# Decode attention on one core: value products into one set of 32 rows, key pieces and value tiles as register loops, the last values in four loads

## The chip, the cores and the metric

The kernel runs on one core of one Trainium2 chip. The metric is the device time of one execution in microseconds (us). A core has five engines that run their own instruction queues and meet at semaphores: PE (matrix products), DVE (vector work), ACT (activations), POOL and SP (here SP only issues transfers, DMAs). PE writes its results to PSUM, a memory of its own, from which DVE and ACT read; the other tiles lie in SBUF.

## The reference, cut to what matters

One token passes a layer of attention over a long cache and then a small MLP. The attention has 32 query heads that share 8 key-value heads (four each), a cache of 16384 tokens, and heads of 128 values, in bf16:

```python
q = (x @ wq).reshape(B, Sq, Hq, Dh).transpose(0, 2, 1, 3)
k = jnp.repeat(k_cache, rep, axis=1)
v = jnp.repeat(v_cache, rep, axis=1)
scores = jnp.einsum("bhqd,bhkd->bhqk", q, k) * (Dh ** -0.5)
p = _softmax(scores, axis=-1)
o = jnp.einsum("bhqk,bhkd->bhqd", p, v)
return o.transpose(0, 2, 1, 3).reshape(B, Sq, Hq * Dh) @ wo
```

`x` is layer-normalised ahead of it and added behind it; the MLP (`w3`, GELU, `w4`) has its own layer norm and its own addition. With one token the shifts in the reference's mixing step leave only zeros, so `w1` and `w2` have no part. The keys and values are 67 MB together, all of which has to be read once; the weights make the rest of the 79 MB.

## The kernel before, in words

**The pairs.** The 8 key-value heads are worked through in 4 pairs (`PAIRS`, L257; the loop at L590). The keys of a pair (8 MB) go to `kb`, in two halves of 64 tokens per partition; its values (8 MB) go to `vb`. Each of these buffers exists once. Partition 64g + u holds 256 neighbouring tokens of head g of the pair.

**Scores.** For each half, DVE transposes the keys from `kb` into `kt` in 8 pieces (`transpose_keys`, L516, the instruction at L520), and PE makes 4 products for each piece (`scores`, L525, L528): 128 columns of a widened query tile `qn` against 512 key columns. A later piece takes the window of `qn` that is shifted by 4 columns, so each piece lands on rows of its own of `s_ps[:, y, :]`, y being the half. PE waits for DVE's count before each piece. The second half's transposes write over the first half's `kt`, piece by piece, once PE has read it.

**Softmax.** `softmax` (L536): DVE takes the maxima (L539), PE turns them (L540), DVE and PE make the bias, ACT computes the exponentials with their sums in `acc` (L550), and DVE transposes these into `pt` (L554, two instructions).

**Values.** `values` (L557) has 64 products (L562): 32 columns of `pt` against 4 tokens x 128 values. Four neighbours (`ct` 0 to 3) go to rows 0, 32, 64 and 96 of one PSUM tile `O_ps[0]`, each over its own 32 columns of the array; 16 such groups are summed up. All wait for the pair's values and for `pt`.

**Gather.** `gather` (L567): a product makes the sums of the exponentials (L570), DVE picks the right block for each row with four masked steps over 128 rows (L575, L578), a product folds them (L581), and DVE divides (L583, L584) into `o_m`.

**Transfers.** All large ones are issued by SP, in the order of the program: `wq`, keys 0, values 0, then for each pair the next keys (pair 1's in one transfer, the others in halves, each once DVE has transposed the half that it overwrites) and the next values (L604, once the last value product has read `vb`). `wo` goes to the first half of `kb`, `w3` and `w4` to the second, after the last keys. The queue serves them in that order.

**PE's program.** Every operation is recorded with its dependencies (`Program.op`, L43), and waits are made from them. DVE, ACT, POOL and SP run their lists straight through (`_run`, L128). PE's list is emitted as a loop over the pairs (`_tensor`, L136): a block for a half, run twice with register `ry` as the half, and a block `pe_rest` for softmax, values and gather. In a half, the 8 pieces with their 32 products are written out one after the other, with a register addition and a wait ahead of each piece (L211), and the branch back at L218. The 64 value products are written out too, behind one wait for the values. After the last pair a branch that is never taken carries a hint to the loop's head (L237). What follows (`wo`, the MLP) is straight.

**The end.** `wo` is multiplied in 32 products (L624), the row is summed and normalised (L633, L396 to L404, L639), `w3` follows in 16 products (L645), GELU and a transpose (L657, L661), `w4` in 56 products (L666), the last addition (L670) and the store (L672).

Of the kernel before, what the change touches and what calls it, by code (L numbers as in the profile page):

```python
# [14 lines left out]
class Op:  # L15
    __slots__ = ("eng", "fn", "deps", "sem", "val", "needed", "dma", "at")

    def __init__(self, eng, fn, deps, dma, at):
        self.eng, self.fn, self.deps, self.dma, self.at = eng, fn, deps, dma, at
        self.sem = self.val = None  # L20
        self.needed = False


class Program:

# [6 lines left out]
    def __init__(self, nc, ctx):  # L32
        self.nc, self.ctx = nc, ctx
        self.ops = {e: [] for e in ("PE", "DVE", "ACT", "POOL", "SP")}
        self.last_w, self.readers, self.users = {}, {}, {}
        self.dma_sems, self.dma_count = {}, {}
        self.mark, self.count = None, {}
        self.y = None
# [4 lines left out]
    def op(self, eng, fn, r=(), w=(), bank=(), dma=None):  # L43
# [23 lines left out]
        o = Op(eng, fn, deps, dma, at)  # L67
# [21 lines left out]
    def emit(self):  # L89
# [8 lines left out]
        for e, ops in self.ops.items():  # L98
            if not any(o.needed and o.dma is None for o in ops):
                continue  # L100
            sem = self.ctx.enter_context(self.nc.semaphore(f"e_{e}"))
            n = 0
            for o in ops:
                if o.dma is None and o.needed:
                    n += 1
                    o.sem, o.val = sem, n
        for e, eng in (("SP", self.nc.sync), ("ACT", self.nc.scalar), ("POOL", self.nc.gpsimd),
                       ("DVE", self.nc.vector)):
            self._run(eng, self.ops[e], {})
        self._tensor()  # L110
# [9 lines left out]
    @staticmethod  # L120
    def _issue(eng, o):
        ins = o.fn(eng)
        if o.dma is not None:
            ins.then_inc(o.sem, 16)
        elif o.needed:
            ins.then_inc(o.sem, 1)
# [8 lines left out]

    def _tensor(self):  # L136
# [7 lines left out]
        half = [k for kind, j, y, k in (a for a in at if a[0] == "half") if (j, y) == (1, 0)]  # L144
        rest = [k for kind, j, k in (a for a in at if a[0] == "rest") if j == 1]
        assert len(at) == pairs * (2 * len(half) + len(rest))
# [3 lines left out]
        def count(o):  # L150
            return max((v for s, v, e in self._wants(o).values() if e == "DVE"), default=0)

        def loads(o):
            return [(s, v) for s, v, e in self._wants(o).values() if e == "dma"]

        vector = next(s for o in loop for s, v, e in self._wants(o).values() if e == "DVE")
        first = {j: at[("rest", j, rest[0])] for j in range(pairs)}
        step = count(first[2]) - count(first[1])

        waits, have = {}, 0  # L160
        for o in (x for x in loop if x.at[1] == 1):
            v = count(o)
            if v > have:
                have = v
                if o.at[0] == "rest" or o.at[2] == 0:
                    waits[o.at[0], o.at[-1]] = v
        steps = [v for (kind, k), v in waits.items() if kind == "half"]
        y_step = count(at[("half", 1, 1, half[0])]) - steps[0]
        have = 0
        for o in loop:  # L170
            kind, j, k = o.at[0], o.at[1], o.at[-1]
            if (kind, k) in waits:
                have = waits[kind, k] + (j - 1) * step + (o.at[2] * y_step if kind == "half" else 0)
            assert count(o) <= have
        last = list(waits.values())[-1]
        assert list(waits)[-1][0] == "rest" and last < steps[0] + step and last - 2 * step > 0
        lead = y_step - (steps[-1] - steps[0])
        assert lead > 0
        need = {k: [at[("rest", j, k)] for j in range(pairs)] for k in rest}
        load = {k: [loads(o) for o in os] for k, os in need.items() if loads(os[0])}  # L180
        assert not any(loads(o) for o in loop if o.at[0] == "half")

        k_load = min(load)
        values = load[k_load]
        assert all(x == values for x in load.values())
        (sem, v0), = values[0]
        gap = values[1][0][1] - v0
        assert all(values[j] == [(sem, v0 + j * gap)] for j in range(pairs)) and v0 >= gap > 0
        seen = {}
        r, rl, rj, ry = (eng.alloc_register(n) for n in ("seen", "landed", "pair", "half"))  # L190
        hint = eng.mark_branch_hint_location()
        eng.reg_mov(r, last - 2 * step)
        eng.reg_mov(rl, v0 - gap)
        eng.reg_mov(rj, 0)
# [4 lines left out]
        now = last - step  # L199
        if steps[0] - lead > now:  # L200
            eng.reg_add(r, r, steps[0] - lead - now)
        now = steps[0] - lead
# [5 lines left out]
        for k in half:  # L208
            v = waits.get(("half", k))
            if v is not None:  # L210
                eng.reg_add(r, r, v - now)  # L211
                eng.wait_ge(vector, r)
                now = v
            self._issue(eng, at[("half", 1, 0, k)])
        self.y = None
        now += y_step
        eng.reg_add(ry, ry, 1)
        eng.br_lt(ry, 2, "pe_half", "pe_rest")  # L218

        nc.switch_bb("pe_rest", parent=None)  # L220
        for k in rest:
            if k == k_load:
                eng.reg_add(rl, rl, gap)
                eng.wait_ge(sem, rl)
            v = waits.get(("rest", k))
            if v is not None:
                eng.reg_add(r, r, v - now)
                eng.wait_ge(vector, r)
                now = v
            self._issue(eng, at[("rest", 1, k)])  # L230
        assert now == last
        eng.reg_add(rj, rj, 1)
        eng.br_lt(rj, pairs, "pe_pair", "pe_leave")


        nc.switch_bb("pe_leave", parent=None)
        eng.br_lt(rj, 0, "pe_pair", "pe_after").branch_hint(hint)  # L237

        nc.switch_bb("pe_after", parent=None)
        seen[id(vector)] = last + (pairs - 2) * step  # L240
        seen[id(sem)] = values[-1][0][1]
        self._run(eng, ops[hi:], seen)

D = 512
HQ = 32
# [12 lines left out]
WHOLE = (1,)  # L258
RPARTS = 6
# [6 lines left out]
def bass_sequential_preLN__gqa_block_cached__mixer_s_mlp__decode_kernel(  # L266
# [13 lines left out]
    with ExitStack() as ctx:  # L280
# [43 lines left out]
        od = sb("od", [128, 128], FP32)  # L324
# [45 lines left out]
        def load_values(j):  # L370
            load("v", vb[:, :], pair_rows(A_v_cache, j), "v")
# [14 lines left out]
        def piece(cuts, m):  # L386
            return [lo <= m < hi for lo, hi in cuts].index(True)

# [60 lines left out]
        load("wq", wq_sb[:, 0:NCH * HQ * DH], A_wq.rearrange("(p k) c -> p (k c)", k=NCH), "v")  # L449
# [47 lines left out]
        for j, (row, key) in enumerate(rows):  # L497
            for k in range(NCH):
                for g in range(2):
# [3 lines left out]
                        start=(k == 0), stop=(k == NCH - 1)), r=["xn", "v"], w=[key], bank=[key])  # L503
# [12 lines left out]
        def transpose_keys(y, ts):  # L516
            for t in ts:
                view = lambda x, t=t: x[:, :].bitcast(I32).rearrange("p (x l w) -> p x (l w)", x=2, l=64)[
                    :, :, t * 512:(t + 1) * 512]
                dve(lambda e, view=view: e.transpose(view(kt), view(kb[y])),  # L520
                    r=[("r", y, n) for n in range(RPARTS)], w=[("kt", t)])

# [183 lines left out]
```

## Time and profile before

| what | us |
|---|---|
| median of three runs | 192.19 (191.9 to 193.25) |
| the profiled execution's own time | 192.09 |
| its span, first to last instruction | 190.8 |
| PE busy | 109.7 (58%) |
| DVE busy | 116.7 (61%) |
| key transposes, 64 | 72.8 |
| score products, 256 | 70.2 |
| value products, 256 | 22.6 |
| bytes read | 79.17 MB, 415 GB/s over the span |

The profile is of one execution. A line of the groups gives source line, engine and operation, output and inputs, shapes and count, then busy time and mean ns of one, then the engine's idle time ahead of them and what ended most of it. PEld is PE's weight load, which overlaps its products; SPq and PEq (PEldq) are the instruction queues. A line of the chain or of the timeline gives start, duration, engine, line and count; in a line of the windows, each engine's busy time is followed by its count, then PE's granted clock, the busy share of the DMA engines (which can pass 1 in short windows) and GB/s. Lines beginning with L and a number are lines of the kernel before.

### The profile page before, as it was taken

What the parts mean: (1) busy time and instruction counts of PE and PEld (TensorE: products, weight loads), DVE (VectorE), ACT (ScalarE), POOL (GpSimd) and SP (SyncE); (2) the same over time, 40 slices, a digit from 0 to 9 for tenths busy, and PEclk for the clock granted to TensorE, in tenths of its full rate; (3) what the DMA queues carried; (4) which work ended last, traced back from release to release, by engine and by line L of the source; (5) the groups of instructions that cost most, each with busy time, mean ns of one, the idle gap of its engine ahead of it and who ended that gap; (6) DMA issues with size and microseconds to landing.
All of it is one profiled execution on the core that took longest, in us unless ns stands there. A gap on an engine that the chain in (4) does not pass through costs nothing.

```text
span 190.8 us, 1799 instructions
## 1 busy us (share of the span) xinstructions
PE 109.7 (58%) x694; PEld 41.3 (22%) x694; DVE 116.7 (61%) x184; ACT 9.1 (5%) x15; POOL 7.4 (4%) x16
## 2 busy tenths in 40 slices
PE   0128099892093006999256599934749896056543
PEld 0113034220031002432013133211313322022213
DVE  7746497984404009998443999935289995503372
ACT  3000000002000000000200000010000000500020
POOL 7100000000000000000000000000000000000041
PEclk9999958999559755899958879995797999558975
DMA  6999999999999999997999999979999899999990
GB/s 227 433 440 440 440 440 441 440 440 440 440 440 440 440 440 440 440 426 344 433 440 440 543 440 426 440 337 440 426 426 488 371 440 398 440 423 411 433 371 20
DMA packets 2612, 79.22 MB, mean 415 GB/s; under 512 B 304, under 2 KB 432, under 8 KB 560
## 3 DMA queue, kind: packets, MB, share of 16 engines
q1 hardware_dynamic: 2600, 79.17, 96.7%
q8 instruction: 2, 0.03, 0.1%
q14 instruction: 2, 0.02, 0.0%
q10 hardware_dynamic: 8, 0.00, 0.0%
HBM read 79.17 MB, written 0.00 MB: 415 GB/s over the span
## 4 chain that ended last, share of the span: by engine, by line
DMA 60%; DVE 32%; PE 5%; issue 1%; ACT 1%; SPq 1%; ACTq 0%
DMA kb<-in_A_k_cache_dram 45%; DVE kt L520 28%; DMA kb<-in_B_w_dram 15%; PE O_ps L562 3%; DVE pt L554 1%; PE mn_ps L666 1%; DVE mx L539 1%; ACT p_sb L550 1%; SPq L355 1%; DVE od L578 1%; PE s_ps L528 1%; PE A_ps L581 0%; PE mn_ps L544 0%; PE mn_ps L540 0%; DVE od L575 0%
## 5 line engine op out<-in xcount | busy, mean ns | idle before, releaser
L528 PE MATMUL s_ps<-kt,qn 128*128 128x512 bf16 x256 | 70.2, 417 | 26.0 <-DVE kt L520 23.9
L520 DVE STREAM_TRANSPOSE kt<-kb 128x1024 int32<-128x1024 int32 x64 | 72.8, 1208 | 15.0 <-DMA kb<-in_A_k_cache_dram 15.0
L528 PEld LDWEIGHTS s_ps<-kt,qn 128*128 128x128 bf16 x256 | 23.5, 104 | 71.9 <-issue 36.6
L562 PE MATMUL O_ps<-vb,pt 128*32 128x512 bf16 x256 | 22.6, 530 | 21.7 <-DMA vb<-in_A_v_cache_dram 13.5
L575 DVE TENSOR_SCALAR od<-O_ps,rowc 128x128 f32<-128x128 f32 x4 | 1.4, 350 | 28.3 <-PE mn_ps L570 28.3
L562 PEld LDWEIGHTS O_ps<-vb,pt 128*32 128x32 bf16 x256 | 8.5, 128 | 34.2 <-issue 23.9
L554 DVE STREAM_TRANSPOSE pt<-p_sb 64x1024 bf16<-64x1024 bf16 x8 | 9.9, 1239 | 5.4 <-ACT p_sb L550 5.3
L550 ACT ACTIVATE p_sb<-s_ps,bias 128x1024 bf16<-128x1024 f32 x4 | 4.5, 1114 | 156.0 <-DVE nmh L546 156.0
L539 DVE TENSOR_REDUCE mx<-s_ps 128x1 f32<-128x1024 f32 x4 | 4.9, 1224 | 4.6 <-PE s_ps L528 4.6
L438 POOL TENSOR_SCALAR st<-st 128x1 f32<-128x1 f32 x1 | 0.2, 242 | 177.4 <-DVE st L423 177.4
L501 PE MATMUL O_ps<-vb,xn 128*64 128x512 bf16 x16 | 3.3, 586 | 5.8 <-DMA vb<-in_A_wq_dram 5.8
L581 PE MATMUL A_ps<-od,zo 128*32 128x128 f32 x8 | 1.6, 285 | 6.4 <-DVE den L583 6.4
L540 PE MATMUL mn_ps<-ident_f,mx 128*1 128x128 f32 x8 | 1.5, 270 | 5.3 <-DVE mx L539 5.3
L578 DVE SCALAR_TENSOR_TENSOR od<-O_ps,rowc,od 128x128 f32<-128x128 f32 x12 | 4.2, 351 | 0.4
L460 DVE CAST ident<-ident_f 4x4 bf16<-4x4 f32 x1 | 3.8, 3849 | 0.6 <-POOL ident_f L455 0.6
L505 DVE STREAM_TRANSPOSE qcol<-O_ps 128x256 f32<-128x256 f32 x4 | 1.6, 428 | 4.0 <-PE O_ps L501 4.0
L463 PE MATMUL O_ps<-x,quarter 4*128 4x128 bf16 x1 | 0.3, 283 | 5.8 <-DVE quarter L461 5.8
L501 PEld LDWEIGHTS O_ps<-vb,xn 128*64 128x64 bf16 x16 | 1.5, 165 | 7.2 <-issue 7.2
L666 PE MATMUL mn_ps<-kb,hcol 128*32 128x128 bf16 x56 | 1.7, 309 | 2.0 <-DMA kb<-in_B_w_dram 2.0
L645 PE MATMUL s_ps<-kb,hc 128*32 128x448 bf16 x16 | 1.7, 572 | 1.4 <-DMA kb<-in_B_w_dram 1.4
L624 PE MATMUL O_ps<-kb,o_b 128*32 128x512 bf16 x32 | 1.9, 380 | 1.1 <-DVE o_b L620 1.1
L584 DVE SCALAR_TENSOR_TENSOR o_m<-A_ps,den,maskdd 32x128 f32<-32x128 f32 x4 | 1.4, 340 | 1.7 <-PE A_ps L581 1.7
(78 smaller groups left out, 45.0 us busy)
## 6 DMA issues: line engine op xcount, KB each, us to landing
kb<-in_A_k_cache_dram SPq DMA_DIRECT2D x6, 4096.0 KB, 23.2
vb<-in_A_wq_dram SPq DMA_DIRECT2D x1, 4096.0 KB, 12.4
kb<-in_A_wo_dram SPq DMA_DIRECT2D x1, 3072.0 KB, 27.0
kb<-in_B_w_dram SPq DMA_DIRECT2D x1, 1792.0 KB, 24.6
kb<-in_B_w_dram SPq DMA_DIRECT2D x1, 1280.0 KB, 27.9
kb<-in_A_wo_dram SPq DMA_DIRECT2D x1, 1024.0 KB, 29.1
kb<-in_B_w_dram SPq DMA_DIRECT2D x1, 384.0 KB, 28.4
kb<-in_B_w_dram SPq DMA_DIRECT2D x1, 128.0 KB, 28.2
```

Source lines behind the costliest of these rows:

```text
L355: P.op(by, lambda e: e.dma_start(dst, src), w=[key, *also], dma=name)
L460: dve(lambda e: e.tensor_copy(ident[:, :], ident_f[0:4, 0:4]), r=["ident_f"], w=["ident"])
L501: pe(lambda e, row=row, k=k, g=g, at=at: e.matmul(row[64 * g:64 * g + 64, :], copies(xn[:, k:k + 1], 64), wq_sb[:, at:at + REP * DH], star ...
L520: dve(lambda e, view=view: e.transpose(view(kt), view(kb[y])), r=[("r", y, n) for n in range(RPARTS)], w=[("kt", t)])
L528: pe(lambda e, n=n, c=c: e.matmul(s_ps[:, bass.ds(P.y, 1), :], qn[:, n, QPAD - 4 * c:QW - 4 * c], ktv[:, n // 2, n % 2, :, 8 * c:8 * c + 8 ...
L539: dve(lambda e: e.tensor_reduce(mx[:, :], s_all, AX.X, ALU.max), r=[("s", 0), ("s", 1)], w=["mx"], **both)
L550: act(lambda e: e.activation(p_sb[:, :], s_all, ACTF.Exp, bias=bias[:, 0:1], scale=float(SCALE), accum_out=acc[:, :]), r=[("s", 0), ("s", ...
L554: dve(lambda e, g=g: e.transpose(pt[64 * g:64 * g + 64, :, :, g, :], p_sb[64 * g:64 * g + 64, :]), r=["p"], w=["pt"])
L562: pe(lambda e, q=q, ct=ct, xl=xl, ch=ch: e.matmul(O_ps[0][32 * ct:32 * ct + 32, :], pt[:, xl, ch, :, :].rearrange("p g u -> p (g u)"), til ...
L578: dve(lambda e, block=block, c=c: e.scalar_tensor_tensor(od[:, :], block, rowc[:, c:c + 1], od[:, :], ALU.mult, ALU.add), r=[key, "rowc", ...
L624: pe(lambda e, r_=r_, q=q: e.matmul(O_ps[0][32 * q:32 * q + 32, :], copies(o_b[:, r_:r_ + 1], 32), wo_sb[:, r_ * D:(r_ + 1) * D], start=(r ...
L666: pe(lambda e, m=m, o=o: e.matmul(n_ps[32 * o:32 * o + 32, 0:128], hcol[:, m, :], w4_sb[:, m, o * 128:(o + 1) * 128], start=(m == 0), stop ...
```

## The change

1. **Value products.** The 64 products of a pair all go into rows 0 to 31 of `O_ps[0]`, summed up one on the other. A clearing product (a zero column against 512 columns) opens the tile, and the product for the sums and the reciprocal move from the gather to ahead of it (`sums`). They are a loop of 16 turns of 4 products in 4 parts; a turn addresses `pt` and `vb` by registers. `od` and the masked steps have 32 rows.
2. **Loads of values.** Pairs 0 to 2 as before, in one transfer; the values of the last pair in 4 transfers of a quarter each. PE waits part by part, not for the transfer itself but for an empty instruction on POOL that waits for it.
3. **Key pieces.** A loop of 8 turns of 4 products, with the window of `qn` and the piece of `kt` addressed by registers, behind a clearing product. DVE transposes two pieces with one instruction (and counts two), except in the second half of the last pair.
4. **Hints.** PE's never-taken branch with its hint moves from behind the loop to the end of PE's program; DVE's program gets one too.
5. **The end.** At four places of what follows the loop, PE makes extra products into an unused PSUM tile (4, 2, 5 and 5, each place a loop of one product a turn).

The diff, cut to its core:

```diff
+    def _vector(self):
+        eng = self.nc.vector
+        rv = eng.alloc_register("never")
+        hint = eng.mark_branch_hint_location()
+        eng.reg_mov(rv, 0)
+        self._run(eng, self.ops["DVE"], {})
+        eng.br_lt(rv, 0, "body", "pe_pair").branch_hint(hint)
...
         nc.switch_bb("pe_half", parent=None)
         self.y = eng.snap(ry, min_val=0, max_val=1)
...
+        eng.wait_ge(vector, r)
+        for a in places("clear", 1, 0):
+            self._issue(eng, at[a])
+        eng.reg_mov(rq, QPAD)
+        eng.reg_mov(rk, 0)
+        eng.br("pe_piece")
+
+        nc.switch_bb("pe_piece", parent=None)
+        self.q = eng.snap(rq, min_val=0, max_val=QPAD)
+        self.k = eng.snap(rk, min_val=0, max_val=8 * (pieces - 1))
+        eng.reg_add(r, r, 1)
+        eng.wait_ge(vector, r)
+        for a in places("key", 1, 0, 1):
+            self._issue(eng, at[a])
+        eng.reg_add(rq, rq, -4)
+        eng.reg_add(rk, rk, 8)
+        eng.br_lt(rk, 8 * pieces, "pe_piece", "pe_halved")
...
+        nc.switch_bb("pe_part", parent=None)
+        eng.reg_add(rl, rl, 1)
+        eng.wait_ge(sem, rl)
+        eng.br("pe_tile")
+
+        nc.switch_bb("pe_tile", parent=None)
+        group = len(places("value", 1, 0, 0))
+        self.t = eng.snap(rt, min_val=0, max_val=group * (parts * tiles - 1))
+        self.z = eng.snap(rz, min_val=0, max_val=64 * (parts - 1) + 2 * (tiles - 1))
+        for a in places("value", 1, 0, 1):
+            self._issue(eng, at[a])
+        eng.reg_add(rt, rt, group)
+        eng.reg_add(rz, rz, 2)
+        eng.reg_alu(ry, rt, group * tiles - 1, ALU.bitwise_and)
+        eng.br_ne(ry, 0, "pe_tile", "pe_apart")
...
-        eng.br_lt(rj, pairs, "pe_pair", "pe_leave")
...
+        eng.br_lt(rj, pairs, "pe_pair", "pe_after")
...
+            nc.switch_bb(f"pe_more{n}", parent=None)
+            assert not o.needed
+            self._run(eng, [o], seen)
+            eng.reg_add(ry, ry, 1)
+            eng.br_lt(ry, o.times, f"pe_more{n}", f"pe_less{n}")
...
+        eng.br_lt(rj, 0, "pe_pair", "pe_end").branch_hint(hint)
...
+MORE = (4, 2, 5, 5)
...
         def load_values(j):
-            load("v", vb[:, :], pair_rows(A_v_cache, j), "v")
+            n = 64 * DH
+            if j < PAIRS - 1:
+                load("v", vb[:, :], pair_rows(A_v_cache, j), ("v", 0),
+                     also=[("v", x) for x in range(1, 4)] + [("landed", x) for x in range(4)])
+                P.op("POOL", lambda e: e.nop(), r=[("v", 0)], w=[("landed", x) for x in range(4)], worth=4,
+                     own="v")
+                return
+            for x in range(4):
+                load(f"v{x}", vb[:, x * n:(x + 1) * n], pair_rows(A_v_cache, j)[:, x * n:(x + 1) * n], ("v", x),
+                     also=[("landed", x)])
+            for x in range(4):
+                P.op("POOL", lambda e: e.nop(), r=[("v", x)], w=[("landed", x)], own="v")
...
+        def more(n):
+
+            P.op("PE", lambda e: e.matmul(O_ps[1][:, :], qb[:, 0, 0, 0:128], kt[:, 0:512], start=True, stop=True),
+                 r=["qb", ("kt", 0)], w=[("O", 1)], bank=[("O", 1)], times=n)
...
-        def transpose_keys(y, ts):
-            for t in ts:
+        def transpose_keys(y, n):
+            for t in range(0, 8, n):
                 view = lambda x, t=t: x[:, :].bitcast(I32).rearrange("p (x l w) -> p x (l w)", x=2, l=64)[
-                    :, :, t * 512:(t + 1) * 512]
-                dve(lambda e, view=view: e.transpose(view(kt), view(kb[y])),
-                    r=[("r", y, n) for n in range(RPARTS)], w=[("kt", t)])
+                    :, :, t * 512:(t + n) * 512]
+                P.op("DVE", lambda e, view=view: e.transpose(view(kt), view(kb[y])),
+                     r=[("r", y, i) for i in range(RPARTS)], w=[("kt", t + i) for i in range(n)], worth=n)
...
+            P.part("clear", j, y)
+            pe(lambda e: e.matmul(s_ps[:, bass.ds(P.y, 1), :], copies(none, 128), copies(none, 512),
+                                  start=True, stop=False, skip_group_check=True),
+               r=["qn"], w=[("s", y)], bank=[("s", y)])
+            for c in range(8):
+                P.part("key", j, y, c)
                 for n in range(4):
-                    pe(lambda e, n=n, c=c: e.matmul(
-                        s_ps[:, bass.ds(P.y, 1), :], qn[:, n, QPAD - 4 * c:QW - 4 * c],
-                        ktv[:, n // 2, n % 2, :, 8 * c:8 * c + 8, :],
-                        start=(c == 0 and n == 0), stop=(c == 7 and n == 3)),
+                    pe(lambda e, n=n: e.matmul(
+                        s_ps[:, bass.ds(P.y, 1), :], qn[:, n, bass.ds(P.q, 128)],
+                        ktv[:, n // 2, n % 2, :, bass.ds(P.k, 8), :],
+                        start=False, stop=(n == 3), skip_group_check=True),
                        r=["qn", ("kt", c)], w=[("s", y)], bank=[("s", y)])
...
         def values(j):
-            tiles = vb[:, :].rearrange("p (x c l d) -> p x l c d", x=4, c=8, l=8)
-            for q in range(16):
-                for ct in range(4):
-                    xl, ch = 2 * q + ct // 2, ct % 2
-                    pe(lambda e, q=q, ct=ct, xl=xl, ch=ch: e.matmul(
-                        O_ps[0][32 * ct:32 * ct + 32, :], pt[:, xl, ch, :, :].rearrange("p g u -> p (g u)"),
-                        tiles[:, xl // 8, xl % 8, 4 * ch:4 * ch + 4, :], start=(q == 0), stop=(q == 15)),
-                       r=["v", "pt"], w=[("O", 0)], bank=[("O", 0)])
+            tokens = vb[:, :].rearrange("p (t d) -> p t d", d=DH)
+            for x in range(4):
+                for it in range(4):
+                    P.part("value", j, x, it)
+                    for n in range(4):
+                        at = 32 * (n % 2) + n // 2
+                        pe(lambda e, n=n, at=at: e.matmul(
+                            O_ps[0][0:32, :], ptv[:, bass.ds(P.t + n, 1), :].rearrange("p o u -> p (o u)"),
+                            tokens[:, bass.ds(P.z + at, 4, step=8), :],
+                            start=False, stop=(n == 3), skip_group_check=True),
+                           r=[("landed", x), "pt"], w=[("O", 0)], bank=[("O", 0)])
+
+        ptv = pt[:, :, :, :, :].rearrange("p x c g u -> p (x c) (g u)")
+
+        def sums(j):
+
+            pe(lambda e: e.matmul(n_ps[0:32, 32:33], zd[:, :], acc[:, :], start=True, stop=True),
+               r=["acc", "zd", "pt"], w=["n"], bank=["mn"])
+            dve(lambda e: e.reciprocal(den[:, :], n_ps[0:32, 32:33]), r=["n"], w=["den"], bank=["mn"])
+            pe(lambda e: e.matmul(O_ps[0][0:32, :], copies(none, 32), copies(none, 512), start=True, stop=False,
+                                  skip_group_check=True), r=["qn"], w=[("O", 0)], bank=[("O", 0)])
...
-                transpose_keys(y, range(8))
-                scores(j, y, range(8))
+                transpose_keys(y, 1 if j == PAIRS - 1 and y else 2)
+                scores(j, y)
...
+            P.part("middle", j)
+            softmax(j)
+            sums(j)
+            values(j)
             P.part("rest", j)
-            softmax(j)
-            values(j)
             gather(j)
```

## The prediction

> **What bounds the kernel now.** I read the page first, then the chain of work in order of time, then one pair's timeline and a few windows of it, and last the rows of PE's own queue.
>
> The page, its slices of DMA, the chain by engine, and the three large groups:
>
> ```profile
> span 190.8 us, 1799 instructions
> ...
> DMA  6999999999999999997999999979999899999990
> ...
> DMA 60%; DVE 32%; PE 5%; issue 1%; ACT 1%; SPq 1%; ACTq 0%
> ...
> L528 PE MATMUL s_ps<-kt,qn 128*128 128x512 bf16 x256 | 70.2, 417 | 26.0 <-DVE kt L520 23.9
> L520 DVE STREAM_TRANSPOSE kt<-kb 128x1024 int32<-128x1024 int32 x64 | 72.8, 1208 | 15.0 <-DMA kb<-in_A_k_cache_dram 15.0
> ...
> L562 PE MATMUL O_ps<-vb,pt 128*32 128x512 bf16 x256 | 22.6, 530 | 21.7 <-DMA vb<-in_A_v_cache_dram 13.5
> ```
>
> The DMA row stands at 9 or near it throughout: the transfers set the end, and engines wait for them (15.0 us of DVE's idle time, 13.5 of PE's). The value products last 530 ns each, yet 256 of them take only 22.6 us: they overlap.
>
> The chain in order of time, pairs 1 and 2 and the end:
>
> ```profile
> 71.89 18.15 DVE kt L520 x16
> ...
> 95.13 1.24 DVE pt L554
> ...
> 97.68 5.49 PE O_ps L562 x63
> ...
> 103.24 0.34 DVE od L575
> ...
> 109.25 14.73 DVE kt L520 x13
> ...
> 124.05 25.39 DMA kb<-in_A_k_cache_dram
> ...
> 159.04 27.88 DMA kb<-in_B_w_dram
> ```
>
> A pair's compute is one serial path: 18.15 us of key transposes, the score tail, the softmax, 5.49 us of value products, the gather, then the next pair's transposes. From the timeline those start at 105.84 for pair 2 and 139.88 for pair 3: 34.0 us per pair. The keys and values of a pair (8.39 MB each) take about 19.4 us each: from 71.89 (keys of pair 1 landed) to 149.44 (last keys landed) four such amounts passed in 77.6 us. So DMA needs 38.8 us per pair and compute 34.0: **compute has 4.8 us per pair to spare**, no more.
>
> The value products of pair 1 in two windows (PE, its loads, clock, DMA), and the spacing of score products at full clock:
>
> ```profile
> 97.67:101.47 3.80, 3.79 (x36) 1.44 (x40) 0.50 0.96 414
> 101.47:103.19 1.72, 1.69 (x32) 0.61 (x24) 1.00 1.24 533
> ...
> 77.52 4.48 PEld L528 LDWEIGHTS s_ps<-kt,qn 128*128 128x128 bf16 x21 [0.28 <-issue]
> ```
>
> The stage starts at half clock and gets the full one 3.8 us later; 40 loads fall in the first window, 24 in the second. The timeline shows groups of four, one group per 0.427 us at half clock: four products, one per quarter of the columns, run abreast. The score products use all columns and so run one by one: 20 gaps in 4.48 - 0.10 us, 0.219 us each at full clock, 0.427 at half.
>
> PE's queue: the back edge, the register work per half and per wait:
>
> ```profile
> L218 PEldq COMPARE_BRANCH  x8: 79/150/245, 32.1 to 158.7; - x8
> L207 PEldq FUSED_REGOPS  x8: 41/41/46, 15.7 to 149.4; - x8
> L211 PEldq ALU_OP  x56: 32/32/36, 24.3 to 157.5; - x56
> ```
>
> A taken branch holds the queue for 220 to 245 ns, one not taken 79. Starts of neighbouring register instructions lie about 0.09 us apart, so a taken branch costs some 0.28 us until the next one runs.
>
> **The change part by part.**
>
> Value products. All 64 of a pair now go into the same 32 rows, so they use the same 32 columns and cannot run abreast. Work on PE: ahead of them come the sums product, moved here from behind them (0.33 us), and a clearing product of 512 columns (0.43 cold). The 3.8 us at half clock then hold 7 products; the other 57 take 57 x 0.218 = 12.4 us, with 0.2 of drain 16.4 us in all. PE's queue may be slower. Each turn of four products needs a copy of its registers (0.09), an address for each of its weights and each of its tokens, the counters (0.1), the branch (0.28) and eight PE instructions (0.1). The trace shows one address computed in the old loop, at 0.09 us. If the two addresses of a product share one such instruction, that is 4 x 0.09 and a turn takes about 0.95; if all come from two, 0.8; if each needs its own, 8 x 0.09 and 1.3. I take 1.0, by the nearest row (one fused instruction already holds several register operations); 0.8 and 1.3 go to the range. The stage is then 0.3 + 15 x 1.0 + 3 x 0.35 (the waits between parts) + 1.15 for the last turn = **17.5 us**, against 5.6 from the end of the transposed probabilities to the first gather step now: +11.9 per pair.
>
> By the Trainium skill, TensorEngine Tiling (Array Packing), section Theoretical Speedup, a product of at most 32 columns gains up to four times from column tiles; taken back, 4 x 5.49 is 22.0 us for this stage, not 17.5. The rows here differ because most of the 5.49 us is at half clock, and a longer stage spends more of itself at full clock.
>
> Key pieces. The same register work per piece: 1.0 us a turn, beside DVE's 1.13 per piece, so it is hidden while a turn stays below that; above it the key stage grows by 16 times the excess. Transposes go two pieces at a time except in the last half: DVE saves at most the fixed part (by 128x256 at 0.428 us and 128x1024 at 1.204, about 0.1 us per instruction dropped, 0.8 per pair) and at least nothing; I take 0.45. But the last transpose now releases two pieces: the score tail after it grows from 1.14 to 2.2 us (a turn more and 0.1 of addresses); in pair 3, to 1.3. The two clears run while PE waits for DVE: nothing; without that cover 0.43 each.
>
> By the Trainium skill, Advanced Engine Details and Errata, section Control Flow Timing, a compare-and-branch takes about 108 ns. The row above has 220 to 245 when taken, and the measurement decides; by the page a turn would be near 0.88 us, the stage PE-bound at 16.4, and the time about 220.
>
> Last values in four pieces. Three more issues of 0.33 us on SP, behind nothing that waits. The pieces would let products start before all has landed, but the probabilities come later than the values (below): nothing gained. The new wait on POOL sits ahead of POOL's work at the end only, which comes long after; its hop adds about 0.15 us where the values land last (POOL's row after DVE: 0.2), pair 0 alone.
>
> Gather: reading 32 rows, not 128, leaves the free size at 128, so 0.35 us each as now; the reciprocal is off the path (-0.1). End: extra products as loops keep the array warm; one turn is one product, one counter and a branch, 0.4 us. The first four run over by 0.25; the others fit into waits of 0.7 to 2.2 us. The 56 last products at full instead of half clock: -0.8. Branch hints: one instruction of 0.05 us at the start and a branch not taken of 0.08: nothing, and unhidden no more than that.
>
> **Sum.** Pair 0: values land at 52.63; products 52.8 to 69.5; gather 2.45, to 72.0; keys of pair 1 landed at 71.89, so nothing is lost. The next values are issued at 69.6 instead of 58.55, and SP's queue shows 1.65 us from a small issue to its landing: just before the keys end. Pair 1: transposes 17.7, tail 2.2, softmax 6.45 (91.17 to 97.63 now), products 17.5, gather 2.45: 46.3 us, so pair 2 starts at 118.3 (now 105.84). Pair 2 the same: pair 3 starts at 164.6 (now 139.88). Pair 3: 18.0 + 1.3 + 6.45 + 17.5, products end at 207.9 (the first gather step now starts at 174.67). DMA runs dry twice, about 110 to 117 and 156 to 164, since values wait for the last product; these transfers still land 8 us ahead of their use, and the weights by about 201, so nothing of that is on the path. The end takes 16.1 us now from that gather step: less 0.1, plus 0.25, less 1.35 (the last weights no longer waited for, and the warm array): 14.9. Span 222.8. The profiled execution took 192.09 with a span of 190.8; with the same 1.3 outside I predict **224 us**. The median shown, 192.19, is its own time within 0.1.
>
> **Rivals.**
> - PE's queue paces both loops. For it: nine addresses per key turn, of which the trace priced only one. From 1.13 us a turn it counts twice. At 1.3 us the stage is 22.0 and the keys take 23.3 to the end of the tail instead of 19.9; pair 0's products end at 74.0, each pair takes 54.2: **253 us**. Against it: fused instructions exist. Chance 0.22.
> - The clock rises with the products done, not with time: 40 of the 64 at half clock as in the row, 40 x 0.427 + 24 x 0.219 = 22.3 us. Pair 0 is late by 5 us and three pairs by 5 each: **244 us**. For it: one window holds 40 loads, the other 24. Against it: the clock rose 3.8 to 4.3 us after the start in score and value stages alike, though the scores had done some 11 of their 64 products by then. Chance 0.08. The 22.0 us by the tiling page above would end at the same time.
> - The array stays warm over the softmax and turns are short: 64 x 0.219 and 0.5: 14.5 us, 3 us less in three pairs: **215 us**. Against it: the clock fell to half in each softmax. Chance 0.09.
> - Not slower: products into the same rows still overlap. It decides where the stage stays below 5.6 + 4.8 = 10.4 us, 0.15 us per product; then DMA hides it all: **192 us**. For it: the DMA row and 4.8 us to spare. Against it: no product in the trace that shares its columns with its neighbour came closer than 0.21 us. Chance 0.03.
>
> **How the numbers follow.** My forecast, 217 to 232, has 0.58. The range takes in the warm case, the late clock and the queue at up to 1.28 us a turn: 212 to 250, leaving out half of the first rival and the last. About 1% is what a measurement can tell here. Faster 0.01 and same 0.02 come from the last rival; slower 0.97.
>
> **What would show it.** Right: L562's successor in about 16 to 18 us per pair, products 0.22 apart or in fours each 1.0 us; transposes of pairs 2 and 3 starting near 118 and 165; two holes in the DMA slices; the chain mostly DVE and PE. Wrong: products less than 0.2 us apart; gaps over 0.3 us between turns in the score stage (then the first rival); a DMA row without holes.

## The result, and the profile after

The changed kernel takes 274.53 us (median of four runs, 273.17 to 275.01) against 192.14 us for the kernel before on the same chip: 1.427 times as long, 95% interval 1.420 to 1.433. That is slower, as predicted, but 50 us past the predicted 224 and 25 past the upper end of the range.

The page of the profiled execution after the change (274.57 us, clock 0.886): span, DMA slices (each a fortieth of the span), chain by engine, and the groups of the value products and the score products.

```profile
span 272.7 us, 3130 instructions
...
DMA  8999999999049979940089989987863994000000
...
PE 52%; DVE 22%; issue 15%; DMA 8%; ACT 2%; SPq 0%; ACTq 0%; DVEq 0%
...
L664 PE MATMUL O_ps<-vb,pt 128*32 x256 | 78.9, 417 | 24.9 <-issue 24.6
L628 PE MATMUL s_ps<-kt,qn 128*128 x256 | 70.9, 416 | 17.1 <-DVE kt L614 11.4
```

DMA went from 60% of the chain to 8%, PE from 5% to 52%, and the DMA row has holes: the transfers now wait for the compute. The value products are busy 78.9 us instead of 22.6. The new word is "issue", 15% of the chain and 24.6 us ahead of the value products alone: PE waits there for nothing that the profile shows, and the rows of its queue, below, say what it does meanwhile.

The chain in order of time shows where (start, duration, what), first in three turns, up to the end of a part, of pair 1's values, then in its keys:

```profile
119.68 1.18 PE O_ps L664 x4
120.86 0.34 issue
121.20 1.20 PE O_ps L664 x4
122.39 0.34 issue
122.74 1.18 PE O_ps L664 x4
123.92 0.91 issue
```

```profile
98.18 1.04 PE s_ps L628 x4
99.22 0.20 issue
99.42 1.04 PE s_ps L628 x4
```

A turn of four value products takes 1.54 us, and 0.57 us more where a new part begins (gap 0.91 instead of 0.34). A turn of four score products takes 1.24 us. The rows of PE's queue for the two products, and for the copy and the branch of the value loop (count, then ns min/median/max):

```profile
L664 PEldq FUSED_REGOPS  x384: 37/58/79, 52.8 to 254.6; - x192
L664 PEldq ALU_OP  x64: 32/36/36, 52.7 to 253.8; - x64
```

```profile
L628 PEldq FUSED_REGOPS  x320: 42/74/84, 25.1 to 221.2; - x160
```

```profile
L279 PEldq FUSED_REGOPS  x64: 84/84/94, 52.5 to 253.7; - x64
```

```profile
L286 PEldq COMPARE_BRANCH  x64: 78/219/231, 53.8 to 255.0; - x64
```

64 value turns have 384 + 64 address instructions: seven a turn, for eight addresses. 64 key turns have 320: five each. The clock is no excuse; two windows of pair 1's value stage (width, then PE busy, PEld busy, DVE, ACT, POOL, granted clock, DMA share, GB/s):

```profile
110.60:114.40 3.80, 3.68 (x11) 1.15 (x11) 0.18 (x2) 0.00 (x0) 0.00 (x0) 0.50 1.00 431
114.40:137.30 22.90, 16.93 (x58) 5.25 (x56) 0.00 (x0) 0.00 (x0) 0.00 (x0) 0.99 0.20 87
```

The clock rises after 3.8 us as before. From then on it is full, and still 22.9 us go by.

Stage by stage, from the timelines of the two kernels (us):

| stage | before | after | predicted |
|---|---|---|---|
| keys, first transpose to maxima, pairs 1 and 2 | 19.28 | 22.75 | 19.9 |
| softmax | 6.45 | 6.45 | 6.45 |
| probabilities to first gather step, pairs 1 and 2 | 5.60, 5.69 | 26.70, 26.86 | 17.5 |
| that step to the next pair's first transpose, pairs 1 and 2 | 2.62, 2.62 | 3.01, 2.79 | 2.45 |
| last pair's first gather step to the end | 16.11 | 17.54 | 14.9 |

### The profile page after: what moved, and what is told of

It is laid out like the page before. It is cut to its first block, busy times and chain, and to the rows that moved or that the text cites. A ratio compares the mean times of both kernels' runs of the same rounds, so it can differ in the third digit from the quotient of the medians.

```text
span 272.7 us, 3130 instructions
## 1 busy us (share of the span) xinstructions
PE 178.4 (65%) x722; PEld 62.2 (23%) x722; DVE 115.0 (42%) x156; ACT 9.0 (3%) x15; POOL 7.4 (3%) x16
## 4 chain that ended last, share of the span: by engine, by line
PE 52%; DVE 22%; issue 15%; DMA 8%; ACT 2%; SPq 0%; ACTq 0%; DVEq 0%
PE O_ps L664 29%; PE s_ps L628 18%; DVE kt L614 12%; DMA kb<-in_A_k_cache_dram 8%; DVE pt L654 4%; DVE mx L639 2%; ACT p_sb L650 2%; DVE od L689 2%; PE O_ps L737 1%; PE A_ps L692 1%; PE O_ps L677 1%; PE O_ps L480 1%; PE mn_ps L644 1%; PE mn_ps L640 1%; DVE od L686 1%
## 5 line engine op out<-in xcount | busy, mean ns | idle before, releaser
L664 PE MATMUL O_ps<-vb,pt 128*32 x256 | 78.9, 417 | 24.9 <-issue 24.6
L628 PE MATMUL s_ps<-kt,qn 128*128 x256 | 70.9, 416 | 17.1 <-DVE kt L614 11.4
L614 DVE STREAM_TRANSPOSE kt<-kb 128x2048 int32<-128x2048 int32 (+1 forms) x36 | 71.0, 2036 | 3.4 <-DMA kb<-in_A_k_cache_dram 2.5
L686 DVE TENSOR_SCALAR od<-O_ps,rowc 32x128 f32<-32x128 f32 x4 | 1.4, 338 | 105.0 <-PE O_ps L664 105.0
L664 PEld LDWEIGHTS O_ps<-vb,pt 128*32 x256 | 25.0, 98 | 79.7 <-issue 78.9
L628 PEld LDWEIGHTS s_ps<-kt,qn 128*128 x256 | 26.3, 103 | 60.7 <-issue 47.0
L639 DVE TENSOR_REDUCE mx<-s_ps 128x1 f32<-128x1024 f32 x4 | 4.9, 1224 | 19.2 <-PE s_ps L628 19.2
L674 PE MATMUL mn_ps<-acc,zd 128*32 128x1 f32 x8 | 1.1, 202 | 16.4 <-DVE pt L654 16.4
L622 PE MATMUL s_ps<-qn 128*128 128x512 bf16 x8 | 3.5, 442 | 5.8 <-DVE qn L702 4.7
L692 PE MATMUL A_ps<-od,zo 32*32 32x128 f32 x8 | 1.8, 314 | 7.1 <-DVE od L689 7.1
L480 PE MATMUL O_ps<-kt,qb 128*128 128x512 bf16 x16 | 5.5, 400 | 0.1
L674 PEld LDWEIGHTS mn_ps<-acc,zd 128*32 128x32 f32 x8 | 0.7, 139 | 16.7 <-DVE pt L654 16.7
L689 DVE SCALAR_TENSOR_TENSOR od<-O_ps,rowc,od 32x128 f32<-32x128 f32 x12 | 4.1, 338 | 0.4
## 6 DMA issues: line engine op xcount, KB each, us to landing
kb<-in_B_w_dram SPq DMA_DIRECT2D x1, 1280.0 KB, 10.3
```

The lines of the kernel that those rows point to most:

```text
L480: P.op("PE", lambda e: e.matmul(O_ps[1][:, :], qb[:, 0, 0, 0:128], kt[:, 0:512], start=True, stop=True), r=["qb", ("kt", 0)], w=[("O", 1)] ...
L614: P.op("DVE", lambda e, view=view: e.transpose(view(kt), view(kb[y])), r=[("r", y, i) for i in range(RPARTS)], w=[("kt", t + i) for i in r ...
L628: pe(lambda e, n=n: e.matmul(s_ps[:, bass.ds(P.y, 1), :], qn[:, n, bass.ds(P.q, 128)], ktv[:, n // 2, n % 2, :, bass.ds(P.k, 8), :], start ...
L639: dve(lambda e: e.tensor_reduce(mx[:, :], s_all, AX.X, ALU.max), r=[("s", 0), ("s", 1)], w=["mx"], **both)
L664: pe(lambda e, n=n, at=at: e.matmul(O_ps[0][0:32, :], ptv[:, bass.ds(P.t + n, 1), :].rearrange("p o u -> p (o u)"), tokens[:, bass.ds(P.z ...
L686: dve(lambda e, block=block: e.tensor_scalar(od[:, :], block, rowc[0:32, 0:1], None, ALU.mult), r=[key, "rowc"], w=["od"], bank=[key])
```

## The experiments

Ratios are to the kernel before on the same chip; the "value stage" is the third row of the table, for pairs 1, 2 and 3.

**e1: both loops written out with constant addresses, all else as changed (still 32 rows).** The theory: the address work on PE's queue makes what lies beyond the prediction. The rival: products that share their columns are slower than 0.218 us each.

```diff
-        self.t = eng.snap(rt, min_val=0, max_val=group * (parts * tiles - 1))
-        self.z = eng.snap(rz, min_val=0, max_val=64 * (parts - 1) + 2 * (tiles - 1))
-        for a in places("value", 1, 0, 1):
-            self._issue(eng, at[a])
...
+        for x in range(parts):
+            eng.reg_add(rl, rl, 1)
+            eng.wait_ge(sem, rl)
+            for it in range(tiles):
+                self.t, self.z = 4 * (tiles * x + it), 64 * x + 2 * it
+                for a in places("value", 1, x, it):
+                    self._issue(eng, at[a])
...
+        for c in range(pieces):
+            self.q, self.k = QPAD - 4 * c, 8 * c
+            eng.reg_add(r, r, 1)
+            eng.wait_ge(vector, r)
+            for a in places("key", 1, 0, c):
+                self._issue(eng, at[a])
```

> Both loops of the changed kernel written out again with constant addresses; products into 32 rows, the moved sums, the loads in pieces and the end stay. Theory A (PE's queue, working out addresses, paces the value loop at 1.54 us and the key loop at 1.24 us a turn): the value stage, from the end of the transposed probabilities to the first gather step, falls from 26.7 to about 16.4 us, the keys with their tail from 22.75 to about 19.8, the time to about 222 us. Theory B (products that share their columns are the main cost, the loops hide beside them): the stage stays at 24 to 27 us and the time near 270.

Measured: 223.56 us, 1.160 times before (1.153 to 1.168). Value stage 17.0, 16.3, 16.2 us, keys 19.67. The chain of pair 1:

```profile
99.05 0.45 PE O_ps L655
99.50 16.21 PE O_ps L642 x64
```

The 64 products follow each other as one piece. So the serial products cost what the prediction made of them, and the other 51 us are the loops'.

**e2 and e3: one loop kept, the other written out as in e1.**

> Value loop kept, key pieces written out with constant addresses. A: keys with tail 22.75 to 19.8 us, value stage 26.7 as it is: about 264 us. B: the keys as they are, 274.

Measured: 263.33 us, 1.366 (1.355 to 1.376); value stage 26.6 in all three pairs, keys 19.66.

> Key loop kept, value products written out with constant addresses, still into 32 rows. A: value stage 16.4 us, keys with tail 22.75: about 231 us. B: 270 or more.

Measured: 232.51 us, 1.206 (1.196 to 1.216); value stage 16.2 to 16.7, keys 22.6 to 22.7. The value loop costs 39.8 us over e1, the key loop 9.0; together 48.7 of the 51. Another 1.5 us lie at the end (17.54 us after the change, 16.05 in e1).

**e4: eight products a turn instead of four, eight turns instead of sixteen.**

```diff
-                for it in range(4):
+                for it in range(2):
-                    for n in range(4):
+                    for n in range(8):
```

> The value loop with 8 products a turn instead of 4, so half the branches, copies and counters, and as many addresses. A, with 0.255 us for the addresses of one product and 0.52 for the rest of a turn: 2.56 us a turn, 8 turns, the value stage 4.1 us shorter (22.6), the time about 258 us. If the branch alone is the cost (0.28 a turn): 2.2 us shorter, 266. B: no change, 274.

Measured: 258.53 us, 1.341 (1.330 to 1.352); value stage 22.85. Queue and chain:

```profile
L664 PEldq FUSED_REGOPS  x448: 37/58/79, 53.0 to 239.1; - x150
L664 PEldq ALU_OP  x32: 32/34/36, 52.8 to 237.2; - x32
```

```profile
124.85 2.20 PE O_ps L664 x8
127.05 0.35 issue
127.40 2.25 PE O_ps L664 x8
```

A turn within a part takes 127.40 - 124.85 = 2.55 us and has 14 + 1 address instructions. Four more products cost 1.01 us and eight instructions: 0.25 us a product, two address instructions and the product's own issue, against 0.218 us for the product on PE. The rest of a turn is 1.54 - 4 x 0.25 = 0.54 us. Fewer turns save only that rest.

**e8: the weights in the value loop at constant addresses.** Every turn weights its values with the first four blocks of probabilities; the work on PE stays, with four addresses less a turn.

```diff
-                            O_ps[0][0:32, :], ptv[:, bass.ds(P.t + n, 1), :].rearrange("p o u -> p (o u)"),
+                            O_ps[0][0:32, :], ptv[:, n:n + 1, :].rearrange("p o u -> p (o u)"),
```

> The changed kernel with its weights in the value loop at constant addresses, the same four for all turns, so that the values are weighted wrongly: four addresses a turn less, one register instruction of about 0.09 us each. A: a turn of 1.54 us takes about 1.18, the value stage 21 us, the time about 251. If the products of a turn are held by something else (their loads not running ahead), the turn stays at 1.5 us and the time near 272.

Measured: 244.05 us, one run; value stage 19.2. Queue and chain:

```profile
L664 PEldq FUSED_REGOPS  x192: 55/55/60, 52.8 to 223.9; - x192
```

```profile
113.36 1.03 PE O_ps L664 x4
114.39 0.02 issue
114.41 1.03 PE O_ps L664 x4
```

Three instructions a turn are left of seven, and the turn falls from 1.54 to 1.06 us: 0.48 us for four, 0.12 us each. The copy at the head of the turn has one register less as well (59 ns, not 84), so 0.11 to 0.12 us is the price of an address. The timelines show the same within a turn: the weight loads start 0.25 to 0.28 us apart after the change (119.65, 119.93, 120.21, 120.46) and 0.15 us apart here (four in 0.54 us, 0.09 us each). That is closer than PE's 0.218 us per product, so here it is only around the branch that the queue holds PE up. The expectation of 1.18 us was too high: an address costs more than its row's 58 ns and the 0.09 us between starts that the prediction used.

**e5 and e6: written out, with four column groups (as before the change) or with two.** All other parts of the change stay; the clearing product and the gather cover 128 and 64 rows. The diff shows e5; e6 has `n % 2`.

```diff
-                            O_ps[0][0:32, :], ptv[:, bass.ds(P.t + n, 1), :].rearrange("p o u -> p (o u)"),
+                            O_ps[0][32 * (n % 4):32 * (n % 4) + 32, :], ptv[:, bass.ds(P.t + n, 1), :].rearrange("p o u -> p (o u)"),
...
```

> Both loops written out and the value products back in four column groups (128 rows in the gather); the moved sums and clears, the key transposes of two pieces, the last values in four loads, the hints and the extra products at the end stay. A: value stage about 6.3 us (5.6 and 0.8 for sums and clear), a pair's compute about 35.2 us, under the 38.8 of its transfers: DMA sets the time again, 191 to 192.2 us. If one of the parts that stay costs something by itself, 193 or more.

Measured: 193.44 us, 1.0055 (1.0031 to 1.008); value stage 6.75, 5.97, 5.89. So e1's 223.56 less 193.44, 30 us, is the price of the shared columns (of the time, beyond what transfers hide). The rest of the change is 1 us slower than before, not equal or faster; e10 to e12 look for that microsecond.

> As e5_flat_4groups, but the value products in two column groups (64 rows), two abreast. The stage should take about 9.5 us, below the 10.4 up to which the prediction says that DMA hides it: 191 to 193.5 us. If there is less to spare than it says (the next values issued too late), DMA runs dry and it takes 195 to 200 us.

Measured: 203.61 us, 1.060 (1.054 to 1.065); value stage 10.34, 9.50, 9.38. This missed: a stage of 10.4 us was to be hidden, and even the 195 to 200 us for less to spare were too low. The transfers do not cover it; the chain runs through all three stages:

```profile
99.29 9.44 PE O_ps L642 x61
...
138.54 8.60 PE O_ps L642 x60
...
176.33 8.48 PE O_ps L642 x61
```

In the kernel before, the timeline shows where compute waits for transfers after pair 1 has started (the bracket is the wait):

```profile
149.46 1.25 DVE L520 STREAM_TRANSPOSE kt<-kb 128x1024 int32<-128x1024 int32 x1 [0.46 <-DMA kb<-in_A_k_cache_dram]
...
168.91 1.04 PE L562 MATMUL O_ps<-vb,pt 128*32 128x512 bf16 x8 [6.76 <-DMA vb<-in_A_v_cache_dram]
```

The first is 0.46 us. Of the second only 168.91 - 166.18 = 2.73 us come after the probabilities. That is 3.2 us once, for pairs 1 to 3 together, and about 1 us more at the last weights. In e6 pair 1 starts 0.4 us later, pairs 1 and 2 take 5.3 and 4.4 us more, pair 3 up to its gather, waits taken out, 3.2 more: 13.3; less 3.2 is 10.1, and the last gather starts 184.83 - 174.67 = 10.2 us later.

**e9: the kernel before with 14 more products behind each pair's values** (zero weights). It doses the stage without any other part of the change.

```diff
+            for _ in range(14):
+                pe(lambda e: e.matmul(O_ps[0][:, :], copies(qn[:, 0, 0:1], 128), copies(qn[:, 0, 0:1], 512),
+                                      start=False, stop=True, skip_group_check=True),
+                   r=["qn", "pt"], w=[("O", 0)], bank=[("O", 0)])
```

> The kernel before with 14 more products behind the values of each pair (zero weights, all 128 columns, into the same tile, so the output is the same): 14 x 0.219 = 3.1 us more in each value stage. Theory of the record: 4.8 us of every pair are hidden by the transfers, so the time stays at 192.1 to 192.6. Theory formed on the two-group kernel: pairs 1 to 3 have one spare of 4.4 us for all of them together (0.46 at the last keys, 2.8 at the last values, 1.1 at w3 and w4 in the profile before), so 3 x 3.1 - 4.4 = 4.9 us come out at the end: 197.0.

Measured: 198.97 us, 1.037 (1.033 to 1.041). The claim of 4.8 us hidden in every pair falls. The new theory is low by 2 us, 1.5 in the profiled execution (198.55), at the end of the kernel. Up to the last gather step 6.1 us of delay have come up, as the stages of pairs 1 to 3 have it (2.9 + 3.2 + 3.3 longer, less 3.2). The 1.1 us expected back at the last weights are more than eaten by `wo`, whose products take 1.27 us longer, at half clock; from that step to the end it is 16.44 us instead of 16.11. The same products in the kernel before and in e9:

```profile
177.70 1.91 PE L624 MATMUL O_ps<-kb,o_b 128*32 128x512 bf16 x32 [1.05 <-DVE o_b L620]
```

```profile
183.82 3.18 PE L628 MATMUL O_ps<-kb,o_b 128*32 128x512 bf16 x32 [1.05 <-DVE o_b L624]
```

**e7: e5 without the extra products at the end** (`more` returns at once).

> As e5_flat_4groups without the extra products at the end. If these save what the prediction took (0.8 us on the 56 last products), this is slower by 0.4 to 0.9 us than e5_flat_4groups; if the last transfer alone sets the end, the same within 0.3.

Measured: 193.66 us, 1.0069 (1.0044 to 1.0095). The interval overlaps e5's: in these kernels the extra products bring and cost nothing that could be measured in the time. They do change the last products: `w4` takes 1.43 us with them (e5) and 1.68 without (e7).

**e10, e11, e12: the hints.** e10 is the kernel before with PE's hint moved and DVE's added as in the change; e11 is e5 with PE's hint behind the loop and none for DVE, as before the change (the diff, against e5); e12 is e11 with DVE's hint put back.

```diff
-        for e, eng in (("SP", self.nc.sync), ("ACT", self.nc.scalar), ("POOL", self.nc.gpsimd)):
+        for e, eng in (("SP", self.nc.sync), ("ACT", self.nc.scalar), ("POOL", self.nc.gpsimd),
+                       ("DVE", self.nc.vector)):
...
-        self._vector()
...
-        eng.br_lt(rj, pairs, "pe_pair", "pe_after")
+        eng.br_lt(rj, pairs, "pe_pair", "pe_leave")
+
+        nc.switch_bb("pe_leave", parent=None)
+        eng.br_lt(rj, 0, "pe_pair", "pe_after").branch_hint(hint)
...
-        eng.br_lt(rj, 0, "pe_pair", "pe_end").branch_hint(hint)
-        nc.switch_bb("pe_end", parent=None)
```

> The kernel before with the hints alone: PE's at the end of its program instead of behind the loop, one more at the end of DVE's. Theory of the record: nothing, 192.4. Rival: the hints make what the flat kernel with four groups has over the kernel before (1.03 us, of which 0.6 lies outside the span and about 0.9 in the landing of the store): 193.0 to 193.5, with 1.9 us outside the span instead of 1.3.

Measured: 191.8 us, 1.0001 (0.9975 to 1.0028); 1.3 to 1.6 us outside the span.

> The flat kernel with four groups, with the hint where it was before (PE's behind the loop, none for DVE); loads in four pieces, merged transposes and extra products stay. Theory of the record: the same as with the hints, 193.4. Rival: without the hints the 1.03 us are gone, 192.2 to 192.6 with 1.3 us outside the span. If it stays at 1.9 us outside, the four loads or the empty POOL instructions have it.

Measured: 191.76 us, 0.9972 (0.9955 to 0.9988), 1.3 us outside the span: the only kernel here that is faster than the one before, by 0.3%.

> The flat kernel with four groups, with the hint at the end of DVE's program kept and PE's hint back behind the loop. If DVE's hint alone makes the 1.7 us between that kernel with both hints (193.44) and with none (191.76), the time is 193.3 to 193.6, with 1.9 us outside the span and about 2 us for the landing of the store; if PE's hint at its new place makes them, or only both together, it is 191.6 to 192.0, with 1.3 us outside and a landing of 1.0 us.

Measured: 193.4 us, 1.0037 (1.0014 to 1.0059), 1.9 us outside the span. SP's wait for the landing of the output, in e11 and in e12:

```profile
SPq L768 <- DMA out_dram<-fin: 1.0, 1, 1.0
```

```profile
SPq L769 <- DMA out_dram<-fin: 2.0, 1, 2.0
```

In the flat kernel DVE's hint makes the output land 1 us later and adds 0.6 us outside the span; by the times that is 1.6 us, by the two ratios 1.2. The landing takes 1.9 to 2.2 us in every kernel from e1 to e8, all of which have the hint. In the kernel before, the hint does neither (e10: landing 1.0 us). What else has to be there for it was not found.

## Why the prediction was wrong, point by point

**DMA bounds; "compute has 4.8 us per pair to spare".** The first half was right. The second was wrong, as e6 and e9 show: comparing 34.0 with 38.8 us per pair overlooks that pair 1 starts only when all its keys have landed, while pair 3 is held only by the second half of its keys. From 71.89 to 149.46 compute does two pairs and half of pair 3's keys, 68.0 + 9.1 us of the 77.6. What is to spare is what the waits show, 3.2 us once. It did not move the 224, which was far past either limit, but the threshold of the last rival (10.4 us) was wrong: 9.4 to 10.3 us of stage cost 6%.

**Value products on PE alone, 16.4 us.** Right: 17.0, 16.3 and 16.2 in e1. Products that share their columns do not overlap: at full clock in e1 they are 0.216 us apart (13 weight loads in 2.69 us). That e1's 223.56 us meets the predicted 224 is partly chance: e1 has no loop, so its stages are 0.5 to 1.3 us shorter than the 17.5 in the sum, and its end (16.05 us for 14.9) and the time outside the span (1.9 us for 1.3) make up for most of it. By the Trainium skill, TensorEngine Tiling (Array Packing), section Theoretical Speedup, products of at most 32 columns gain up to four times from column tiles. The runs stay within that: the stage of e1 is 2.5 to 2.8 times that of e5.

**The turn of PE's queue, "I take 1.0", bounds 0.8 and 1.3.** This is the step that failed: 1.54 us. It had three errors, the first two in the addresses. The prediction let both addresses of a product share an instruction, four a turn, because one fused row held several register operations; the queue has seven a turn (e4: two for each added product). It priced one at 0.09 us, the distance between starts of neighbouring register instructions; e8 measures 0.11 to 0.12. Seven of them are about 0.8 us instead of 0.36. And what else is in the turn takes 0.7 to 0.8 us instead of 0.57; no row had shown its share for the eight PE instructions, 0.1. The gap between parts is 0.57 instead of 0.35. The stage is then 15 x 1.54 + 3 x 0.57 + 1.16 = 26.0 us from the first product, 26.7 with the sums and the clearing ahead of it, for 17.5 predicted. The upper bound failed too: it counted eight instructions, but at 0.09. The branch was priced rightly: 219 ns when taken, 78 when not. The Trainium skill, Advanced Engine Details and Errata, section Control Flow Timing, gives about 108 ns for a compare-and-branch, which neither value of that row bears out.

**Key turn 1.0 us, "hidden while a turn stays below" 1.13.** The same error: 1.24 us, though with five address instructions where the first rival counted nine addresses. The condition was right in that the stage grows above DVE's pace; 16 x 0.11 = 1.8 us by that rule. e3 shows 3.0 us a pair over e1. DVE is not held up (first to last transpose 17.64 us after the change, 17.66 in e1); all of the growth lies behind the last transpose, where PE has four whole turns left: 104.18 - 99.07 = 5.1 us to the maxima, predicted 2.2, and 2.0 in e1, without the loop. What makes the 1.2 us above the rule was not separated.

**Transposes two at a time, 0.45 us a pair.** Right: from first to last 17.64 us instead of 18.14, 0.06 us for each of the eight instructions dropped. (The two rows give a fixed part of 0.17 us, not the 0.1 that was worked out from them.) The tail after the last transpose takes more than that back, as said: in e1, without the loops, the keys take 19.67 us instead of 19.28.

**Last values in four pieces, nothing gained.** Right as far as shown: e5 and e11 keep them, and neither gains more than 0.3%.

**The end, 14.9 us.** 17.5. `w4` was shorter (1.05 instead of 1.71 us), as said, and e5 against e7 bears out that the extra products help there. But the clock fell to half just as `wo` began (3.25 us instead of 1.91), as in e9 where there are no extra products, and the output landed in 1.9 us instead of 1.0, which e12 gives to the hint in the flat kernel.

**Hints, nothing.** Wrong by 1.6 us in the flat kernel (e11 against e12), right for the kernel before (e10).

**The sum and the rivals.** The order of the work was right. The misses, stage by stage: 9.2 to 9.4 us in each of the four value stages (37.0), 2.85 us in the keys of pairs 1 and 2 and 3.5 in those of pair 3 (9.1), 1.1 from the gathers to the next keys, 2.6 at the end, 0.6 outside the span. These 50.4 us carry 224 to the 274.5 measured, within 0.1. What happened is the first rival, "PE's queue paces both loops". Its sign, gaps over 0.3 us between turns in the score stage, did not come: they are 0.20, and even the rival's own 1.3 us a turn would have left 1.3 - 1.04 = 0.26. The gaps over 0.3 are in the value stage (0.34). The rival's 253 us were too low, mostly for a value stage of 22.0 us where 26.7 were measured: four times 4.7 us. Two holes in DMA came, but not the two predicted at 110 to 117 and 156 to 164 us: no bytes move from 71 to 79 us, where pair 0's longer stage holds up the next values, and from 120 to 138, the first of the predicted ones, later and longer. The second of them did not come, because SP issues the last values quarter by quarter from 176.24 us on, while pair 2's products still run: from 176 to 196 us 339 GB/s move. The late clock and the warm array did not come: the value stage of pair 1 starts at half clock and has the full one after 3.8 us, with 8 of its 64 products started.

## What to carry to other kernels

Before a written-out run of products becomes a loop, count the addresses that a register sets: here each cost 0.11 to 0.12 us on the queue and each product had two, which with its issue is more than the 0.218 us that the product takes (0.25, e4). By these figures only a longer product would hide them; none was tried. Read what a transfer hides from the waits that are there (3.2 us once), not from the difference of two rates per stage. When a change has several parts, price the one with the unknown row by its worst case in count and in unit together, and carry that to the range.

## What the runs showed of the hardware

- A turn of four products with constant weights takes 1.06 us, against 4 x 0.218 = 0.87 on PE; with both addresses in registers 1.54 us.
- At the start of `wo`, a gather after the last value product, PE ran at half clock in some kernels (`wo` took 3.25 us after the change, 3.18 in e9) and at full clock in others (1.91 before, in e1 and in e2). The length of the stage ahead does not decide it, since e2's 26.6 us are the same as after the change; what does is open.
- A never-taken branch with a hint at the end of DVE's program cost 1.6 us (1.2 by the ratios) in one kernel and nothing in another.
- Loops over products in four column groups with register addresses were not tried.
